# Linear attention and two MLPs on one core: 1 KB pieces for the loads of k and the first q

## The chip, the cores and the metric

The kernel runs on one core of one Trainium2 chip. The metric is device time in microseconds (us). The kernel before took 1558.11 us, the median of three runs that lay between 1558.07 and 1558.21. One execution of it was profiled.

## The reference

The kernel computes three layers for 8 batches of 576 tokens, 4608 tokens in all:

```python
kv  = np.einsum('bhsd,bhse->bhde', k, v)          # 8 batches, 8 heads, 576 tokens, head size 64
out = np.einsum('bhsd,bhde->bhse', q, kv)
rms = np.sqrt(np.mean(out * out, axis=-1, keepdims=True) + 1e-06)
x   = (out / rms * g_norm)                        # regrouped to x[4608, 512]
h   = x @ w_in                                    # first MLP, d_ff = 2048
g   = np.where(h >= 1, h, np.where(h <= -1, 0.0, (h + 1) ** 2 / 4.0))
x   = g @ w_out
h   = x @ w_in2                                   # second MLP
r   = np.maximum(h, 0.0)
return (r * r) @ w_out2
```

Inputs are float32, except that the weights lie in memory as 64-bit floats, which the kernel reads as pairs of 32-bit integers and narrows itself.

## The kernel before

**Layout.** Activations are held transposed: features on the 128 partitions, tokens along the row. d_model = 512 is 4 chunks of 128, d_ff = 2048 is 16 chunks of 128, counted f = 0 to 15. A pair of heads (hp = 0 to 3) fills 128 partitions and is one chunk of x. A batch has 512 tokens in its main block and 64 left over. Tile names give layer, batch or chunk: x_0_3 is x of batch 0, pair 3; ph_0_4 is the product x·w_in of batch 0 for chunk f = 4; u_0_4 and gs_0_4 are what the activation makes of it; acc_0_2 is the third of the four output accumulators of batch 0; raw_0_7 and raw_1_7 are the loads of chunk 7 of w_in and of w_out (in the order's names raw1_0_0 is layer 1's, w_in, chunk 0).

**Precision.** A product of float32 values is done as three products of halves (hi·hi, hi·lo, lo·hi; mm3, L237). So every weight passes, after its load of 512 KB, through `narrow_w` (ACT Prelu L267, DVE shift L269, DVE combine L270) and `split_halves` (ACT cast L216, DVE subtract L184): on ACT two, on DVE three instructions of 512 columns for each chunk. x is split likewise (ACT L216, DVE L229), and so is the activation's result (gs, ACT L216 and DVE L229).

**The first 120 us.** All queues start empty. SP issues the loads of k, v and q of batch 0 pair by pair, with weights raw_0_0 and raw_0_1 between pairs 1 and 2. It issues in program order; each of its DMAs takes one of eight landing semaphores in turn, and waits until the DMA eight places ahead has landed. For each pair `kv_stage` forms kᵀv on PE (pkv, L478), `t_first` transposes q by PE (pt, L499 for the main blocks, L501 for the left-over tokens) and DVE copies it out (qT, L218); `o_first` makes q·kv (po, L510; ACT square L511; DVE L210), `r_first` the norm (pr, L533; ACT Ln L534 and Exp L536; several DVE steps; x split L216, L229). `keep_warm` (L1146) puts products on a dummy tile between these. After that the main loop runs over seven batches and 16 chunks f: `h_stage` (ph; ACT relu L704, ACT square L223, DVE L706 to u), `g_stage` (gs) and `out_stage` (acc). Batches 1 to 7 have their attention woven into the loop: DVE transposes their q (L552), PE does pkv (L478), po (L568) and pr (L600).

**Banks.** In batch 0, ph of the chunks f = 2 to 5 sits in the PSUM banks of the accumulators acc_0_0 to acc_0_3. The first product of acc_0_c therefore waits until DVE (L706) has read ph_0_(c+2) for u_0_(c+2).

**What sets the order.** Up to about 714 us the order on each engine is not that of the code: a scheduler arranges the instructions by its own reckoning of when their inputs are there. Loads on SP keep their program order up to small shifts. From there to the end runs the second MLP with a reduced number of products (L877), in an order that the code fixes.

**The places of the change.** `load_kv` loads k and v of every batch and pair in one DMA each of 256 KB. Partition p holds the tokens 4p to 4p+3 of both heads. v lies on the partition as (head, token, 64): four tokens of a head follow each other in memory and on the partition. k lies as (token, head, 64), so that a token's two heads are 128 contiguous columns. `load_first` lays q of batch 0 out as k. In `t_first` one transposition then takes a token index c of both heads, 128 columns, at once.

Of the kernel before, what the change touches and what calls it, by code (L numbers as in the profile page):

```python
# [76 lines left out]
def linear_attention_rms_two_mlps(  # L77
# [12 lines left out]
    nc = tc.nc  # L90
    B, H, S, D = q.shape
    NT, DM = out.shape
    DFF = w_in1.shape[1] // 2
    P = 128
# [3 lines left out]
    TB = 512  # L98
    MR = TB // P
# [86 lines left out]
    ident = ap2.tile([P, P], F32, tag="q", name="ident")  # L186
# [218 lines left out]
    def load_kv(b, hp):  # L405
        h0 = 2 * hp
        if b > 0:

            r = rests[turn[b, hp] % len(rests)]
            kvr[b, hp] = (r[:, 0], r[:, 1])  # L410
        for n, src in enumerate((k, v)):
            pool, tag = (ep, "e") if (b, hp) == (0, NP - 1) else (st, "st")
            t = pool.tile([P, TB], F32, tag=tag, name=f"{'kv'[n]}_{b}_{hp}")
            rows = src[b, h0 : h0 + 2, :TB, :].rearrange("h (p r) d -> p h r d", r=MR)
            if n == 0:

                t = t.rearrange("p (r h d) -> p r h d", h=2, r=MR)
                nc.sync.dma_start(t, rows.rearrange("p h r d -> p r h d"))
            else:
                t = t.rearrange("p (h r d) -> p h r d", h=2, r=MR)  # L420
                nc.sync.dma_start(t, rows)
            kvm.setdefault((b, hp), []).append(t)
            if b > 0:
                rest = src[b, h0 : h0 + 2, TB:, :].rearrange("h p d -> p h d")
                nc.sync.dma_start(kvr[b, hp][n][:REM], rest)
# [14 lines left out]
    def load_first():  # L440


        left = wp.tile([REM, 2, H, D], F32, tag="w0_7", name="kvr0")
        qr = wp.tile([REM, H, D], F32, tag="w1_6", name="qr0")
        for hp in range(NP):
            load_kv(0, hp)
            heads = slice(2 * hp, 2 * hp + 2)
            kvr[0, hp] = (left[:, 0, heads, :], left[:, 1, heads, :])
            pool, tag = (ep, "e") if hp == NP - 1 else (st, "st")
            t = pool.tile([P, TB], F32, tag=tag, name=f"q_0_{hp}")  # L450
            t = t.rearrange("p (c h d) -> p c h d", h=2, c=MR)
            rows = q[0, 2 * hp : 2 * hp + 2, :TB, :].rearrange("h (p c) d -> p c h d", p=P)
            nc.sync.dma_start(t, rows)
            qs[0, hp] = [t[:, c] for c in range(MR)] + [qr[:, heads, :]]
            if hp == 1:
                for f in range(2):
                    load_w(1, f, 0)
            if hp == 0:
                for d, src in ((left[:, 0], k), (left[:, 1], v), (qr, q)):
                    nc.scalar.dma_start(d, src[0, :, TB:, :].rearrange("h p d -> p h d"))  # L460
                for j in range(2):
                    nc.scalar.dma_start(
                        gvec[j * D : (j + 1) * D, :], g_norm.rearrange("(d o) -> d o", o=1)
                    )

    def kv_stage(b, *hps):
        ps = bank(b, f"pkv_{b}_{hps[0]}")
        for n, hp in enumerate(hps):
            kt, vt = kvm.pop((b, hp))
            r = kvr.pop((b, hp))  # L470


            for c in range(MR + 1):
                for j in range(2):
                    s = slice(j * D, (j + 1) * D)
                    d = slice(n * P + j * D, n * P + (j + 1) * D)
                    lhs, rhs = (kt[:, c, j], vt[:, j, c, :]) if c < MR else (r[0][:, j], r[1][:, j])
                    nc.tensor.matmul(ps[s, d], lhs, rhs, start=c == 0, stop=c == MR)  # L478
        for n, hp in enumerate(hps):
            for j in range(2):  # L480
                s = slice(j * D, (j + 1) * D)
                d = slice(n * P + j * D, n * P + (j + 1) * D)
                if b == 0:
                    copy(engine("kv_hi", b), kv0[s, hp, s], ps[s, d])
                    continue
                if (b, hp) in WHOLE:
                    copy(engine("kv_hi", b), kvw[s, hp % 2, s], ps[s, d])
                    continue
                t = kvbd[turn[b, hp] % len(kvbd)]
                copy(engine("kv_hi", b), t[s, 0, s], ps[s, d])  # L490
                nc.vector.tensor_tensor(t[s, 1, s], ps[s, d], t[s, 0, s].bitcast(F32), ALU.subtract)

    def t_first(hp):
        qT = scratch(hp, "qT")
        q5 = qs[0, hp]
        for half in range(2):
            ps = bank(0, f"pt_0_{hp}_{half}")
            for c in range(2):
                nc.tensor.transpose(ps[:, c * P : (c + 1) * P], q5[2 * half + c], ident)  # L499
            rest = slice(half * (REM // 2), (half + 1) * (REM // 2))  # L500
            nc.tensor.transpose(ps[:, 2 * P : U], q5[MR][rest], ident[rest, rest])  # L501
            copy(engine("q_hi", 0), qT[:, half], ps[:, :U])
        hl[0, hp] = qT
# [774 lines left out]
```

## Time and profile before

| | |
|---|---|
| median of three runs | 1558.11 us |
| profiled execution | 1558.01 us |
| its span | 1556.1 us (1.9 us lie around it) |
| PE busy | 1546.0 us, 99% of the span |
| DVE busy | 1134.4 us, 73% |
| ACT busy | 975.8 us, 63% |
| DMA | 327,520 packets, 368.23 MB, mean 237 GB/s; 196,976 packets under 512 bytes |
| loads of k (main blocks) | 32 of 256 KB |
| loads of q of batch 0 | 4 of 256 KB |

Times are microseconds from the start of the span. An engine's busy time counts its own instructions; PEld, the load of stationary operands, runs beside PE. The chain of waits follows the work that ended last back to the start and says by which engine each stretch of it was set. In the timeline a bracket behind an instruction gives the idle time ahead of it on its engine and what ended this.

### The profile page before, as it was taken

The page shows a single profiled execution, that of the slowest core. Times are in us where ns is not written, and L with a number is a line of the kernel's source. Part 1 is how long each engine was busy: PE and PEld are TensorE (multiplying, and loading weights), DVE is VectorE, ACT ScalarE, POOL GpSimd, SP SyncE. Part 2 cuts the span into 40 slices and gives each one's busy share as a digit, 9 for nine tenths or more (in the row PEclk, how much of TensorE's full clock was granted, in tenths as well). Part 3 has the DMA queues.
Part 4 walks back from the last instruction along what each step waited for, and adds up shares of the span by engine and source line. Part 5 has one row for each costly group of instructions (what it writes and reads, how often), then busy time and mean ns, then how long its engine had stood idle before and what let it go on. Part 6 is the DMA issues. An engine that isn't in the chain of part 4 may idle for free.

```text
span 1556.1 us, 22351 instructions
## 1 busy us (share of the span) xinstructions
PE 1546.0 (99%) x7727; PEld 1283.7 (82%) x7729; DVE 1134.4 (73%) x2000; ACT 975.8 (63%) x1833; POOL 20.4 (1%) x38
## 2 busy tenths in 40 slices
PE   9999999999999999999999999999999999999999
PEld 5787888888888888888888888888888888888898
DVE  6986886877877786754587558778965596568666
ACT  5977766767666676765575466456646663666364
POOL 0000000000000000000000000000000000000000
PEclk9999999999999999999999999999999999999999
DMA  9666899996877967935676877696876676877797
GB/s 288 193 220 187 273 321 281 303 312 197 273 250 239 284 208 228 294 95 173 192 245 196 221 218 248 197 239 197 259 224 206 209 235 198 241 252 217 209 333 310
DMA packets 327520, 368.23 MB, mean 237 GB/s; under 512 B 196976, under 2 KB 222576, under 8 KB 327408
## 3 DMA queue, kind: packets, MB, share of 16 engines
q1 hardware_dynamic: 295360, 308.60, 66.8%
q10 hardware_dynamic: 32048, 58.20, 10.0%
q8 instruction: 61, 1.00, 0.3%
q14 instruction: 51, 0.42, 0.1%
HBM read 282.59 MB, written 84.15 MB: 236 GB/s over the span
## 4 chain that ended last, share of the span: by engine, by line
PE 97%; ACT 1%; DVE 1%; DMA 1%; issue 0%; SPq 0%; DVEq 0%; ACTq 0%
PE po L877 27%; PE ph L877 27%; PE acc L237 20%; PE ph L237 19%; PE pkv L478 1%; PE po L237 1%; PE pr L600 1%; DMA v<-in_v_dram 0%; PE pwarm L1146 0%; ACT raw L267 0%; ACT w L216 0%; DMA ws<-wsd 0%; PE pr L533 0%; DVE t L518 0%; DVE w L184 0%; PE po L510 0%
## 5 line engine op out<-in xcount | busy, mean ns | idle before, releaser
L877 PE MATMUL ph<-x,ws 128*128 128x512 f32 (+1 forms) x2016 | 422.6, 371 | 0.7 <-DMA ws<-wsd 0.7
L877 PEld LDWEIGHTS ph<-x,ws 128*128 128x128 f32 x2016 | 355.9, 188 | 66.4 <-DVE h L934 0.9
L877 PE MATMUL po<-t,ws 128*128 128x512 f32 x1680 | 381.6, 389 | 0.0
L877 PEld LDWEIGHTS po<-t,ws 128*128 128x128 f32 x1680 | 315.4, 188 | 65.4
L237 PE MATMUL ph<-x,w 128*128 128x512 f32 x1344 | 329.4, 392 | 1.2 <-ACT w L216 0.5
L237 PEld LDWEIGHTS ph<-x,w 128*128 128x128 f32 x1344 | 248.8, 188 | 54.1 <-ACT w L216 1.4
L806 DVE TENSOR_TENSOR t<-g,t 128x512 fp32r<-128x512 f32 (+1 forms) x288 | 183.6, 643 | 90.1 <-ACT t L216 84.5
L216 ACT CAST t<-g 128x512 fp32r<-128x512 f32 (+1 forms) x288 | 166.6, 585 | 101.8 <-DVE t L806 49.6
L237 PE MATMUL acc<-gs,w 128*128 128x512 f32 x696 | 173.0, 392 | 1.6 <-DVE u L706 1.6
L237 PE MATMUL acc<-gs,wt 128*128 128x512 f32 x648 | 157.9, 391 | 0.0
L237 PEld LDWEIGHTS acc<-gs,w 128*128 128x128 f32 x696 | 128.6, 188 | 27.8 <-DVE u L706 2.0
L934 DVE TENSOR_TENSOR h<-ph,e 128x512 f32<-128x512 f32 (+1 forms) x144 | 92.8, 646 | 68.3 <-PE ph L877 60.8
L237 PEld LDWEIGHTS acc<-gs,wt 128*128 128x128 f32 x648 | 120.1, 188 | 24.3
L704 ACT ACTIVATE u<-ph,halfb 128x512 f32<-128x512 f32 x112 | 77.3, 691 | 91.2 <-PE ph L237 88.7
L706 DVE SCALAR_TENSOR_TENSOR u<-u,ph 128x512 f32<-128x512 f32 x112 | 76.4, 682 | 53.6 <-ACT u L223 53.1
L941 ACT ACTIVATE h<-h 128x512 f32<-128x512 f32 (+1 forms) x120 | 70.3, 586 | 63.0 <-DVE h L934 58.3
L927 DVE TENSOR_TENSOR e<-ph,e 128x512 f32<-128x512 f32 (+1 forms) x96 | 61.3, 644 | 48.3 <-PE ph L877 47.4
L229 DVE TENSOR_TENSOR gs<-u,gs 128x512 fp32r<-128x512 f32 x112 | 76.9, 687 | 22.8 <-ACT gs L216 22.2
L216 ACT CAST gs<-u 128x512 fp32r<-128x512 f32 x112 | 69.8, 623 | 37.8 <-DVE u L706 34.7
L942 ACT ACTIVATE g<-h 128x512 f32<-128x512 f32 (+1 forms) x120 | 70.7, 589 | 3.2
L223 ACT ACTIVATE u<-u 128x512 f32<-128x512 f32 x112 | 70.9, 633 | 1.2 <-ACT u L704 0.3
L216 ACT CAST x<-xr 128x512 fp32r<-128x512 f32 (+1 forms) x84 | 49.1, 585 | 35.0 <-DVE xr L857 17.6
(134 smaller groups left out, 1533.0 us busy)
## 6 DMA issues: line engine op xcount, KB each, us to landing
ws<-wsd SPq DMA_DIRECT2D x336, 512.0 KB, 4.3
wsd<-s ACTq DMA_DIRECT2D x96, 512.0 KB, 4.9
wt<-wsd SPq DMA_DIRECT2D x54, 512.0 KB, 5.5
raw<-in_moe_w_in_dram SPq DMA_DIRECT2D x32, 512.0 KB, 6.0
raw<-in_moe_w_out_dram SPq DMA_DIRECT2D x32, 512.0 KB, 6.3
xr<-x1d SPq DMA_DIRECT2D x36, 256.0 KB, 4.8
out_dram<-ov SPq DMA_DIRECT2D x142, 64.0 KB, 3.7
wsd<-w SPq DMA_DIRECT2D x17, 512.0 KB, 4.7
```

The source lines that it names most:

```text
L216: return e.copy(dst, src)
L223: e.activation(dst, src, AF.Square)
L229: lo = engine(op + "_lo", phase).tensor_tensor(t[:, 1, :], src, t[:, 0, :].bitcast(F32), ALU.subtract)
L237: nc.tensor.matmul(dst, wt(a), xt(c), start=first and n == 0, stop=last and n == 2)
L704: nc.scalar.activation(u, ps, AF.Relu, bias=halfb, scale=0.5)
L706: nc.vector.scalar_tensor_tensor(u, u, 1.0, ps, op0=ALU.min, op1=ALU.max)
L806: engine2(op + "_lo").tensor_tensor(t[:, 1, :], src, t[:, 0, :].bitcast(F32), ALU.subtract)
L877: nc.tensor.matmul(ps, wt(a), xt(c), start=first and n == 0 and i == 0, stop=last and n == len(lhs) - 1 and i == 2, skip_group_check=True,)
L927: nc.vector.tensor_tensor(e[i, p], bank, e[i, 1], ALU.add)
L934: nc.vector.tensor_tensor(h, bank, add, ALU.add)
L941: nc.scalar.activation(u, h, AF.Relu)
L942: nc.scalar.activation(g, u, AF.Square)
```

## The change

k of all batches and q of batch 0 are laid out as v: (head, token, 64). A DMA of them is then made of pieces of 1 KB (four tokens of one head) where it was made of pieces of 256 bytes (one token of one head). The products for kᵀv take their stationary operand from the new place; there are as many as before, of the same shape. In `t_first` the two heads of a token are no longer next to each other; 16 transpositions of 128x128 (4 pairs, 2 halves, 2 token indices) become 32 products with the identity as moving operand, one for each head, with 64 columns of q stationary and an output of 64 partitions by 128. The left-over tokens are transposed as before.

```diff
@@ load_kv
-            if n == 0:
-                t = t.rearrange("p (r h d) -> p r h d", h=2, r=MR)
-                nc.sync.dma_start(t, rows.rearrange("p h r d -> p r h d"))
-            else:
-                t = t.rearrange("p (h r d) -> p h r d", h=2, r=MR)
-                nc.sync.dma_start(t, rows)
+            t = t.rearrange("p (h r d) -> p h r d", h=2, r=MR)
+            nc.sync.dma_start(t, rows)
@@ load_first
-            t = t.rearrange("p (c h d) -> p c h d", h=2, c=MR)
-            rows = q[0, 2 * hp : 2 * hp + 2, :TB, :].rearrange("h (p c) d -> p c h d", p=P)
+            t = t.rearrange("p (h c d) -> p h c d", h=2, c=MR)
+            rows = q[0, 2 * hp : 2 * hp + 2, :TB, :].rearrange("h (p c) d -> p h c d", p=P)
             nc.sync.dma_start(t, rows)
-            qs[0, hp] = [t[:, c] for c in range(MR)] + [qr[:, heads, :]]
+            qs[0, hp] = [t[:, :, c] for c in range(MR)] + [qr[:, heads, :]]
@@ kv_stage
-                    lhs, rhs = (kt[:, c, j], vt[:, j, c, :]) if c < MR else (r[0][:, j], r[1][:, j])
+                    lhs, rhs = (kt[:, j, c, :], vt[:, j, c, :]) if c < MR else (r[0][:, j], r[1][:, j])
@@ t_first
-                nc.tensor.transpose(ps[:, c * P : (c + 1) * P], q5[2 * half + c], ident)
+                for j in range(2):
+                    d = slice(j * D, (j + 1) * D)
+                    src = q5[2 * half + c][:, j]
+                    nc.tensor.matmul(ps[d, c * P : (c + 1) * P], src, ident, start=True, stop=True)
```

The new code also moves instructions that it does not name. The second MLP's part is in the same order as before; the part under the scheduler is not. Line numbers of the new kernel are a few lower: L704 there is L706 here, L550 is L552, L516 is L518, L519 and L520 are L521 and L522, L473 is L478, L566 is L568, L598 is L600.

First place: the start of DVE, behind its memsets. pt_0_0_0 and pt_0_0_1 are the two halves of the first pair's transposed q in PSUM, kv0 the copy of kᵀv, d1_0_0 the first step on the first weight chunk. Before:

```order
L218 COPY qT_0_0_235<-pt_0_0_0_236 128x288
L218 COPY kv0_126<-pkv_0_0_222 64x64 x2
L1159 TENSOR_SCALAR gvec_122<-gvec_122 128x1
L218 COPY qT_0_0_235<-pt_0_0_1_241 128x288
L218 COPY kv0_126<-pkv_0_1_252 64x64 x2
L210 TENSOR_SCALAR o_0_0_283<-po_0_0_1_288,gvec_122 128x288
L269 TENSOR_SCALAR d1_0_0_297<-raw1_0_0_151 128x512
```

And now:

```order
L269 TENSOR_SCALAR d1_0_0_305<-raw1_0_0_151 128x512
L218 COPY kv0_126<-pkv_0_0_222 64x64 x2
L1157 TENSOR_SCALAR gvec_122<-gvec_122 128x1
L218 COPY qT_0_0_235<-pt_0_0_0_236 128x288
L218 COPY qT_0_0_235<-pt_0_0_1_243 128x288
L218 COPY kv0_126<-pkv_0_1_256 64x64 x2
```

The first weight step stands ahead of all of the first pair's copies, where six of these stood ahead of it.

Second place: DVE around gs_0_2 and u_0_4, some 55 us into the run; d and w with two numbers are weight chunks on their way, d_1_5 of w_out and d_0_7 of w_in. Before:

```order
L706 SCALAR_TENSOR_TENSOR u_0_2_654<-u_0_2_654,ph_0_2_641 128x512
L552 STREAM_TRANSPOSE qT_0_565<-q_0_558 128x576
L184 TENSOR_TENSOR w_1_4_638<-d_1_4_635,w_1_4_638 128x2x256
L229 TENSOR_TENSOR gs_0_2_671<-u_0_2_654,gs_0_2_671 128x512
L269 TENSOR_SCALAR d_1_5_677<-raw_1_5_520 128x512
L706 SCALAR_TENSOR_TENSOR u_0_3_696<-u_0_3_696,ph_0_3_683 128x512
L270 SCALAR_TENSOR_TENSOR d_1_5_677<-raw_1_5_520,d_1_5_677 128x512
L706 SCALAR_TENSOR_TENSOR u_0_4_780<-u_0_4_780,ph_0_4_767 128x512
```

And now, the end of that stretch:

```order
L269 TENSOR_SCALAR d_1_6_777<-raw_1_6_606 128x512
L519 SCALAR_TENSOR_TENSOR t_0_728<-t_0_728,wk_1_0_579 128x576
L184 TENSOR_TENSOR w_0_7_638<-d_0_7_635,w_0_7_638 128x2x256
L269 TENSOR_SCALAR d_0_8_681<-raw_0_8_632 128x512
L520 TENSOR_TENSOR t_0_728<-wk_1_0_580,t_0_728 128x576
L270 SCALAR_TENSOR_TENSOR d_0_8_681<-raw_0_8_632,d_0_8_681 128x512
L270 SCALAR_TENSOR_TENSOR d_1_6_777<-raw_1_6_606,d_1_6_777 128x512
L229 TENSOR_TENSOR x_1_0_716<-t_0_728,x_1_0_716 128x512
L184 TENSOR_TENSOR w_0_8_684<-d_0_8_681,w_0_8_684 128x2x256
...
L184 TENSOR_TENSOR w_1_6_780<-d_1_6_777,w_1_6_780 128x2x256
...
L704 SCALAR_TENSOR_TENSOR u_0_4_796<-u_0_4_796,ph_0_4_783 128x512
```

u_0_4 stood four places behind gs_0_2 (the last row shown of before) and stands 20 places behind it now, with work on the weight chunks 5 to 9 and on the norm of batch 1's first pair in between.

Third place: PE from the middle of the first accumulators. Before:

```order
L237 MATMUL acc_0_1_849<-gs_0_0_587,w_1_0_494 128x512 x3
L237 MATMUL acc_0_1_849<-gs_0_1_625,w_1_1_501 128x512
L237 MATMUL acc_0_2_850<-gs_0_0_587,w_1_0_494 128x512 x3
L237 MATMUL acc_0_1_849<-gs_0_1_625,w_1_1_501 128x512 x2
L237 MATMUL acc_0_2_850<-gs_0_1_625,w_1_1_501 128x512 x3
```

And now:

```order
L237 MATMUL acc_0_1_865<-gs_0_2_687,w_1_2_531 128x512 x3
L473 MATMUL pkv_1_746<-v_1_586,k_1_583 64x64 x8
L473 MATMUL pkv_1_746<-rest_128 64x64 x2
L566 MATMUL po_1_0_837<-qT_1_761,kvw 128x288
L566 MATMUL po_1_1_850<-qT_1_761,kvw 128x288
L237 MATMUL ph_0_7_992<-x_0_0_217,w_0_7_638 128x512 x3
...
L598 MATMUL pr_1_0_966<-wk_1_1_759,ones 128x288
L598 MATMUL pr_1_1_969<-wk_1_1_759,ones 128x288
L237 MATMUL acc_0_2_866<-gs_0_0_603,w_1_0_510 128x512 x3
```

Between acc_0_1 and acc_0_2, PE now does the attention of batch 1's second pair and the four groups of three products of ph_0_7 (the first of the four groups is shown); the same rows stood later before.

## Rows read from the trace of the kernel before

**Rows 1.** Chain of waits, shares by engine.

```profile
PE 97%; ACT 1%; DVE 1%; DMA 1%; issue 0%; SPq 0%; DVEq 0%; ACTq 0%
```

**Rows 2.** Windows: us, PE, PEld, DVE, ACT, POOL busy; clock, DMA, GB/s.

```profile
0.00:50.00 50.00, 46.08 (x265) 29.13 (x267) 36.41 (x83) 32.43 (x63) 3.68 (x14) 1.00 0.94 274
10.00:40.00 30.00, 28.12 (x165) 18.31 (x167) 25.57 (x56) 21.21 (x43) 1.75 (x4) 1.00 0.99 308
...
150.00:200.00 50.00, 50.00 (x263) 41.30 (x263) 39.68 (x75) 37.07 (x75) 2.18 (x3) 1.00 0.85 267
```

**Rows 3.** PE timeline, 52 to 68 us: start, duration, engine, work, idle before.

```profile
54.31 0.96 PE L237 MATMUL acc<-gs,w 128*128 128x512 f32 x3 [1.56 <-DVE u L706]
57.81 4.27 PE L237 MATMUL acc<-gs,w 128*128 128x512 f32 x17
```

**Rows 4.** Timelines of DVE and ACT in the first 40 us.

```profile
10.06 0.46 DVE L218 COPY qT<-pt 128x288 f32<-128x288 f32 x1 [7.89 <-PE pt L501]
...
20.10 0.78 ACT L536 ACTIVATE y<-y,expb 128x576 f32<-128x576 f32 x1
...
39.82 0.68 DVE L229 TENSOR_TENSOR x<-t,x 128x512 fp32r<-128x512 f32 x1
```

**Rows 5.** DMA by window: weights 10.3 to 12.3, then k, 15.6 to 16.4.

```profile
DMA packets 652, 0.65 MB, mean 326 GB/s; under 512 B 15, under 2 KB 652, under 8 KB 652
...
DMA packets 780, 0.20 MB, mean 249 GB/s; under 512 B 776, under 2 KB 780, under 8 KB 780
```

**Rows 6.** SP timeline, 7 to 18 us: two issues of two loads.

```profile
7.78 0.92 SPq L249 DMA_DIRECT2D raw<-in_moe_w_in_dram  x2
...
16.27 1.24 SPq L249 DMA_DIRECT2D raw<-in_moe_w_in_dram  x2
```

**Rows 7.** DMA issues at 7.8, 16.3, 17.0 us: KB, us to landing.

```profile
raw<-in_moe_w_in_dram SPq DMA_DIRECT2D x1, 512.0 KB, 4.9
...
raw<-in_moe_w_in_dram SPq DMA_DIRECT2D x1, 512.0 KB, 6.4
...
raw<-in_moe_w_in_dram SPq DMA_DIRECT2D x1, 512.0 KB, 8.1
```

**Rows 8.** DVE timeline, 53 to 66 us.

```profile
53.58 0.68 DVE L706 SCALAR_TENSOR_TENSOR u<-u,ph 128x512 f32<-128x512 f32 x1
54.18 0.77 DVE L552 STREAM_TRANSPOSE qT<-q 128x576 f32<-128x576 f32 x1
54.87 0.65 DVE L184 TENSOR_TENSOR w<-d,w 128x512 fp32r<-128x512 f32 x1
55.44 0.68 DVE L229 TENSOR_TENSOR gs<-u,gs 128x512 fp32r<-128x512 f32 x1
56.04 0.42 DVE L269 TENSOR_SCALAR d<-raw 128x512 int32<-128x512 int32 x1
56.38 0.68 DVE L706 SCALAR_TENSOR_TENSOR u<-u,ph 128x512 f32<-128x512 f32 x1
...
61.17 0.82 DVE L518 SCALAR_TENSOR_TENSOR t<-pr,t 128x288 f32<-128x288 f32 x2 [0.69 <-ACT t L223]
62.02 0.76 DVE L521 SCALAR_TENSOR_TENSOR t<-t,wk 128x576 f32<-128x576 f32 x1
62.70 0.68 DVE L229 TENSOR_TENSOR gs<-u,gs 128x512 fp32r<-128x512 f32 x1
```

**Rows 9.** Pieces of the critical chain, 40 to 80 us: start, duration, work.

```profile
62.08 0.73 PE pkv L478 x20
...
65.99 0.97 PE po L568 x4
...
72.45 0.97 PE pr L600 x4
73.43 2.76 PE ph L237 x12
```

**Rows 10.** Groups by line, PE to 56 us: busy and mean ns, idle before.

```profile
L499 PE MATMUL pt<-ident,q 128*128 128x128 f32 x16 | 3.5, 290 | 0.0
```

## Prediction

> **What bounds the kernel now.** I read the chain of waits first: PE sets 97% of it [rows 1]. So the time changes only where PE waits or does more. The windows say where that is. From 150 us on PE is busy 50.00 of 50 us with DVE at 39.68 and ACT at 37.07; in the first 50 us it is busy 46.08, and between 10 and 40 us DVE has 25.57 busy us of 30 [rows 2]. The front is thus a race of DVE, ACT and DMA to give PE its first x and weights, and PE fills it with dummy products, so that its busy share there is no measure of use. Then the PE timeline around the first accumulators shows the one large late wait: 1.56 us at 54.31, ended by DVE's u [rows 3]. That is u_0_2, whose ph holds the bank of acc_0_0. Last I read DVE's timeline around it: one instruction behind the other, no idle time [rows 8]. DVE is the engine to watch, and the change moves instructions on it.
>
> **Terms.** The sum is made on the profiled execution, 1558.01 us (span 1556.1 plus 1.9), 0.1 below the median of the runs.
>
> *1. Loads.* A window inside a weight load, pieces of 1 KB, moves 326 GB/s; one inside a load of k, pieces of 256 bytes (776 of 780 packets under 512 bytes), 249 GB/s [rows 5]. A load of 256 KB takes 1.05 us at 249 and 0.80 at 326, 0.25 less. Batch 0 has four of k and four of q: 2.0 us less in the first 19 us, and 1.0 us less (two of each) ahead of the first weight raw_0_0. Packets fall by 36 loads times 768 = 27,648. The other 28 loads of k lie under a PE that is never idle [rows 2]: worth nothing.
> raw_0_0 lands at 7.78 + 4.9 = 12.7 us [rows 6, 7], so at 11.7 afterwards. I credit none of the 2.0 us by itself, because what follows is DVE's queue, which takes its own time (term 2); the bounds of the credit are 0 and −2.0.
> The Trainium skill agrees on the direction: "DMA: Bandwidth & Descriptors", section "Why small descriptors are slow (HBM only)", puts 11 cycles on a 256-byte piece, 8 of them for data. By that page a load would gain 1.05 x (1 − 8/11) = 0.29 us, eight of them 2.3 us, as an estimate; the rows' 0.25 is used.
>
> *2. DVE's start.* Before, DVE begins the first pair's copies at 10.06 and ends x_0_3 at 39.82 + 0.68 = 40.50 [rows 4]. Now the first weight step stands first, so DVE stands until raw_0_0 is there, 11.7, with the first copies behind it, and po_0 and pr_0 of PE behind these. From there DVE has the same 25.6 busy us [rows 2]: 37.3 without a wait. Following the new order I find two places where DVE must wait: about 1.5 us ahead of the copy of the third kᵀv (its product stands on PE behind pr of the first pair and two dummy products), and about 1.8 us ahead of the second pair's norm (ACT stands at the weights raw_0_2 and raw_0_3 first). Together 40.6 to 40.7 where it was 40.50: +0.2. These two waits are estimates from the order and the durations; a wait that does not come gives −3, one that doubles +3, and DVE's 4.4 idle us of 30 in 10 to 40 us are there to swallow either.
>
> *3. acc_0_0.* A transposition of 128x576 (one for each later pair of heads) now stands ahead of u_0_2 on DVE; start to start it costs 0.69 (54.18 to 54.87) [rows 8]. u_0_2 ended at 54.26 [rows 8]; now 54.26 + 0.2 + 0.69 = 55.15. So acc_0_0 starts at about 55.2 instead of 54.31, which by itself would be +0.9. But PE has in the meantime po and pr of batch 1's first pair out of the way, 2 x 0.97, as the later ones of the same shapes [rows 9], which it did before between 54.31 and 57.81.
>
> *4. acc_0_2.* PE now does 13 products of acc_0_0 and acc_0_1 (4.27/17 = 0.25 each as listed, 0.23 start to start: 2.76/12 [rows 3, 9]): 55.2 + 3.0 = 58.2. Five products with gs_0_2 follow (DVE has that at 55.15 plus u_0_3 and the two steps on a weight chunk and gs itself, 0.60 + 0.34 + 0.60 + 0.60 = 57.3): 1.15. Then pkv 0.73, po 0.97, the twelve of ph_0_7 2.76, pr 0.97 [rows 9]; PE stands at acc_0_2 at 58.2 + 6.6 = 64.8.
> acc_0_2 needs u_0_4. On DVE it is the 20th behind gs_0_2. Start to start [rows 8]: eleven of 512 columns with two operands at 0.60 are 6.6, four shifts at 0.34 are 1.4, the transposition 0.69, the two halves of the first norm step 0.82, two of 576 columns 1.35 (0.68 for one, 62.02 to 62.70): 10.8. u_0_4 is done at 57.3 + 10.8 = 68.1. PE waits 3.3 us.
> PE has then done 18 products of acc, pkv, po, pr and ph_0_7 and stands at 68.1. Before, it had six products of acc done at 57.81 [rows 3], and the same set would be complete at 57.81 + 12 x 0.23 + 0.73 + 0.97 + 2.76 + 0.97 = 66.0. So **+2.1 us** for terms 2 to 4. Since DVE stays full behind u_0_4 and PE has nothing it could do faster, I take it to stay to the end. Bounds: if u_0_4 is early, PE is not held at all and has at 64.8 what before it had at 66.0, −1.2; if DVE also waits for ACT on the way (the row of that norm step shows 0.69 of it [rows 8]) or runs later by the waits of term 2, up to +4.
> What hid u_0_4 before was its place four behind gs_0_2; that cover is gone. Behind the waiting acc_0_2 on PE stands all the rest of the batch, and no other engine can use the time: DVE is the one waited for.
>
> *5. More products on PE.* 16 transpositions become 32 products. The rows have 16 transpositions at 290 ns, 4.6 us in sum, 3.5 without overlap [rows 10]. No row has the new shape. The nearest is pkv: ten products of 64 moving columns in 0.73 us [rows 9], 0.073 each; with 128 columns twice that, 0.146, and 32 of them 4.7 us. So +0.1 to +1.2; were the two heads to run side by side, 2.3 us, a gain of 2.2. I take 0 for the end time, since they lie before 28 us where dummy products and waits for DVE surround them; without that cover it is what stands here.
>
> Sum: 1558.01 + 0 (loads) + 2.1 (terms 2 to 4) + 0 (term 5) = **1560.1 us**.
>
> **Rivals.** 0.2% of the time, 3.1 us, is about what a measurement of this kernel can tell from no change.
> *The saving shows.* The start is bound by the loads, x_0_3 comes earlier by what the pieces save, and the reordering is worth nothing: 1558.0 − 2.0 = 1556.0. For it: DMA engines are 99% busy from 10 to 40 us [rows 2]. Against it: DVE is 25.57 of 30 busy there, and the time at which a weight lands is not the time at which DVE gets to it. With a shorter norm chain on top it could pass −3.1. The Trainium skill is on this side: "Perfetto Trace Analysis", section 'What "DMA-bound" means', says that for such kernels large descriptors are what matters. By that rule the 2.0 us come back; the row of DVE speaks against its case being this one.
> *ACT held by loads (slower).* In the new order ACT takes raw_0_2 and raw_0_3 ahead of Ln and Exp of the second pair. They land at 16.27 + 6.4 = 22.7 and 17.0 + 8.1 = 25.1 [rows 6, 7], less 2.0: 20.7 and 23.1. Exp then starts not before 23.7, where a comparable one starts at 20.10 [rows 4]: +3.6, of which term 2 has 0.2. If neither DVE's idle time nor the dummy products absorb it, 1558.0 + 2.1 + 3.4 = 1563.5. It decides from the point where 4.4 idle us of DVE [rows 2] are used up.
> *Nothing.* u_0_4 comes by a shorter way than I sum, or PE makes the 2.1 us good out of small waits behind: 1558.0, give or take 0.7.
> *Dear products.* If a float32 product with the identity costs four times the transposition, 16 x 3 x 0.29 = 13.9 us more of PE in the first 28 us, up to 1571.9 if none is hidden. The pkv row speaks against it. The Trainium skill has the ratio: "TensorE: Matmul & The Clock Gate", section "Terms", calls the transposing mode 4 times faster for float32. No run here shows that yet.
> That the pieces do not change is excluded: the load's tile and source both run (head, token, 64) now.
>
> **How the numbers follow.** Forecast 0.43, the saving shows 0.16, ACT held 0.22, nothing 0.16, dear products 0.03. The likeliest's own range is 1558.8 to 1561.6. The range for eight in ten goes from 1555.9, the saving's time, to 1563.6, that of ACT held; some two in ten lie beyond. Faster by over 0.2% (under 1555.0): 0.08, half of the saving's case. Slower by over 0.2% (over 1561.2): nearly all of ACT held, the dear products, and a sixth of the forecast's case: 0.32. Within: 0.60.
>
> **What would show it.** DVE's first instruction behind its memsets is the step on raw_0_0, with its wait ended by ACT or a DMA at 11 to 13 us; PE idles some 3 us ahead of acc_0_2 between 60 and 70 us, ended by DVE's u (line 704 of the new kernel); u_0_2 ends at about 55; packets are 27,648 fewer; from 150 us on PE is busy 50 of 50 as before. I am wrong if PE has no such wait or has its largest elsewhere, if the start of acc_0_0 moves by over 2 us, or if the new products have more than 6 us in the trace.

## The result and the profile after

The changed kernel takes 1569.53 us, the median of runs between 1568.02 and 1572.88, where the kernel before took 1558.07 beside it: 1.0083 times as long, 95% interval 1.0071 to 1.0094. The forecast was 1560.1 with a range to 1563.6. The profiled execution has a span of 1567.5 us, 11.4 more than before.

The chain of waits of the kernel after, by engine [rows 1]:

```profile
PE 94%; DMA 3%; ACT 2%; DVE 1%; issue 0%; SPq 0%; ACTq 0%; DVEq 0%
```

PE's share of the chain was 97%. The three points are no measure of the time lost, because the chain also follows a DMA while PE is still at work. PE's windows say where time is lost; first three stretches as in [rows 2], then the rest of the first two layers (PE, PEld, DVE, ACT, POOL busy, granted clock, DMA share, GB/s):

```profile
0.00:50.00 50.00, 46.38 (x305) 29.73 (x306) 34.66 (x80) 30.81 (x61) 3.28 (x14) 1.00 0.96 314
10.00:40.00 30.00, 29.43 (x209) 18.88 (x208) 23.59 (x53) 20.78 (x42) 0.71 (x3) 1.00 0.98 325
150.00:200.00 50.00, 50.00 (x265) 41.66 (x264) 38.09 (x71) 34.38 (x69) 2.81 (x2) 1.00 0.94 292
150.00:400.00 250.00, 246.39 (x1286) 204.49 (x1285) 189.83 (x353) 169.27 (x337) 9.32 (x11) 0.99 0.88 276
400.00:720.00 320.00, 317.43 (x1642) 263.80 (x1641) 224.11 (x410) 209.43 (x414) 4.56 (x10) 0.99 0.70 219
```

The last two rows of the kernel before:

```profile
150.00:400.00 250.00, 250.00 (x1310) 207.68 (x1310) 196.74 (x365) 176.11 (x351) 7.95 (x11) 1.00 0.89 280
400.00:720.00 320.00, 320.00 (x1659) 266.25 (x1658) 226.53 (x413) 210.62 (x415) 6.37 (x9) 1.00 0.74 227
```

A PE that was never idle between 150 and 720 us now is, 3.6 and 2.6 us. Idle time is not all, so I compare progress: at the time t at which PE of the kernel before has done a certain number of columns (without the dummy products, the transpositions of the front and the narrow products for kᵀv), how much later has this kernel done as many? This is the lag. Up to 150 us it also moves with the order of the work itself (with the products for kᵀv counted in, it is 3.8 at 100 us, not 4.5), so where the order is a new one the readings rest on 200 us and later.

```
us later than before, at t =   25   40   60   70  100  200  250  275  490  515 1200
kernel after                  0.5  4.0  0.4  4.3  4.5  2.0  2.0  7.4  7.5 11.9 12.3
```

The front costs 2.0 us by 200 us. Two places behind it cost 5.4 (at 260 us) and 4.4 (at 500). Near the end 0.9 comes back, since a wait of 0.72 us of the kernel before at 1500 us is gone.

PE of the kernel after at these two places, the first and then the second (start, duration, idle before and what ended it):

```profile
259.35 1.29 PE L237 MATMUL acc<-gs,w 128*128 128x512 f32 x5
264.25 0.40 PE L237 MATMUL po<-qT,kvbd 128*128 128x288 f32 x1 [3.61 <-ACT qT L216]
264.49 1.00 PE L237 MATMUL acc<-gs,w 128*128 128x512 f32 x2
...
502.43 0.40 PE L237 MATMUL po<-qT,kvbd 128*128 128x288 f32 x1 [2.57 <-ACT qT L216]
```

Both times q·kv of a later batch stands at ACT's cast of its transposed q, with the accumulators' products queued behind it. At 260 us ACT itself stood. Its timeline:

```profile
260.14 0.60 ACT L216 CAST s<-s 128x512 fp32r<-128x512 f32 x1
263.12 0.37 ACTq L176 DMA_DIRECT2D wsd<-s  x1
263.53 0.67 ACT L216 CAST qT<-qf 128x576 fp32r<-128x576 f32 x1 [2.79 <-DMA wsd<-w]
```

And the chain there:

```profile
252.49 10.56 DMA wsd<-w
...
263.07 0.02 ACTq L176
```

wsd are stores of prepared second-MLP weights. ACT issues one; its landing semaphore was last used by a store that SP issued at 252.49 and that landed at 263.05; ACT stands until then, and the cast that PE needs is behind the store. In the kernel before that cast stands ahead of the store, and PE does the same po without a wait (ACT, then PE):

```profile
256.24 0.68 ACT L216 CAST qT<-qf 128x576 fp32r<-128x576 f32 x1 [0.85 <-DVE qf L557]
257.59 0.37 ACTq L176 DMA_DIRECT2D wsd<-s  x1
...
257.84 0.29 PE L237 MATMUL po<-qT,kvbd 128*128 128x288 f32 x1
```

At 500 us it is DVE: the transposition qf stands behind work on a weight tile wf.

```profile
491.02 5.18 DMA wf<-wsd
...
496.29 0.69 DVE wf L340
...
500.90 0.78 DVE qf L555
```

In the kernel before DVE does the transposition ahead of its step on that tile:

```profile
489.95 0.77 DVE L557 STREAM_TRANSPOSE qf<-q 128x576 f32<-128x576 f32 x1
...
499.25 0.69 DVE L340 TENSOR_TENSOR wf<-wf 128x512 f32<-128x512 f32 x1 [2.21 <-DMA wf<-wsd]
```

After the pause PE is also slower for a while. Windows directly behind it, and a little later:

```profile
264.30:267.50 3.20, 3.20 (x10) 2.55 (x11) 2.60 (x4) 3.20 (x8) 0.00 (x0) 0.54 1.08 386
268.00:272.00 4.00, 4.00 (x21) 3.35 (x20) 1.37 (x2) 1.83 (x5) 0.00 (x0) 1.00 0.88 235
```

A granted clock of 0.54, about the lower level of 1.2 GHz, for some 3.2 us: ten products are listed in them, and 21 in the 4.0 us a little later. By this clock I estimate some 1.5 us on top of the 3.6 of waiting, 5.1 of the 5.4 in all.

The front: DVE's start [rows 4] and what ends its waits:

```profile
11.72 0.43 DVE L269 TENSOR_SCALAR d<-raw 128x512 int32<-128x512 int32 x1 [9.55 <-DMA raw<-in_moe_w_in_dram]
13.21 0.15 DVE L1157 TENSOR_SCALAR gvec<-gvec 128x1 f32<-128x1 f32 x1 [0.70 <-DMA gvec<-in_g_norm_dram]
20.96 0.22 DVE L218 COPY kv<-pkv 64x64 f32<-64x64 f32 x1 [2.40 <-PE pkv L473]
41.84 0.69 DVE L229 TENSOR_TENSOR x<-t,x 128x512 fp32r<-128x512 f32 x1
```

PE around the first accumulators [rows 3, 9], DVE's u_0_2 (the third u of the batch) and u_0_4 [rows 8], and the new products [rows 10]; these are 64 records, two for each of the 32:

```profile
56.97 4.39 PE L237 MATMUL acc<-gs,w 128*128 128x512 f32 x18
61.28 0.69 PE L473 MATMUL pkv<-v,k 128*64 128x64 f32 x16
62.61 1.24 PE L566 MATMUL po<-qT,kvw 128*128 128x288 f32 x4 [0.52 <-ACT kvw L216]
63.77 3.29 PE L237 MATMUL ph<-x,w 128*128 128x512 f32 x12
68.71 1.24 PE L598 MATMUL pr<-wk,ones 128*128 128x288 f32 x4 [1.65 <-ACT wk L208]
70.10 6.21 PE L237 MATMUL acc<-gs,w 128*128 128x512 f32 x26 [0.16 <-DVE u L704]
```

```profile
56.23 0.68 DVE L704 SCALAR_TENSOR_TENSOR u<-u,ph 128x512 f32<-128x512 f32 x1
...
69.37 0.68 DVE L704 SCALAR_TENSOR_TENSOR u<-u,ph 128x512 f32<-128x512 f32 x1
```

```profile
L497 PE MATMUL pt<-ident,q 128*64 128x128 f32 x64 | 5.7, 286 | 0.0
```

The transfers [rows 5 to 7]. A window from 12 to 14 us, with loads of k, v and q and the end of a weight load, now moves 379 GB/s, where one inside a load in pieces of 256 bytes moved 249. It is the best of those read: three windows from 5 to 11 us move 315 to 330. From 5 to 16 us as a whole it is 348 GB/s, where it was 298. SP's weight issues start at 5.01 and 13.21 instead of 7.78 and 16.27:

```profile
DMA packets 853, 0.76 MB, mean 379 GB/s; under 512 B 113, under 2 KB 853, under 8 KB 853
```

```profile
5.01 2.75 SPq L249 DMA_DIRECT2D raw<-in_moe_w_in_dram  x2
...
13.21 0.92 SPq L249 DMA_DIRECT2D raw<-in_moe_w_in_dram  x2
```

The packets fall to 299,873, by 27,647.

### The profile page after: what moved, and what is told of

It is laid out like the page before. It is cut to its first block, busy times and chain, and to the rows that moved or that the text cites. A ratio compares the mean times of both kernels' runs of the same rounds, so it can differ in the third digit from the quotient of the medians.

```text
span 1567.5 us, 22414 instructions
## 1 busy us (share of the span) xinstructions
PE 1551.6 (99%) x7777; PEld 1288.4 (82%) x7777; DVE 1134.3 (72%) x2000; ACT 973.7 (62%) x1833; POOL 19.1 (1%) x38
## 2 busy tenths in 40 slices
DMA packets 299873, 368.24 MB, mean 235 GB/s; under 512 B 160112, under 2 KB 194928, under 8 KB 299760
## 4 chain that ended last, share of the span: by engine, by line
PE 94%; DMA 3%; ACT 2%; DVE 1%; issue 0%; SPq 0%; ACTq 0%; DVEq 0%
PE po L875 27%; PE ph L875 27%; PE acc L237 18%; PE ph L237 17%; PE po L237 1%; PE pkv L473 1%; DMA x1d<-ev 1%; PE pr L598 1%; DMA wsd<-w 1%; DMA k<-in_k_dram 0%; ACT w L216 0%; ACT raw L267 0%; DMA wf<-wsd 0%; DMA gvec<-in_g_norm_dram 0%; ACT u L702 0%; PE pwarm L1144 0%
## 5 line engine op out<-in xcount | busy, mean ns | idle before, releaser
L704 DVE SCALAR_TENSOR_TENSOR u<-u,ph 128x512 f32<-128x512 f32 x112 | 76.4, 682 | 50.3 <-ACT u L223 49.9
```

The costliest lines, as they stand in the source:

```text
L704: nc.vector.scalar_tensor_tensor(u, u, 1.0, ps, op0=ALU.min, op1=ALU.max)
```

## Experiments

My theory: the two pauses come from the order in which the scheduler now writes the work behind 200 us; the pieces and the products as such cost little. One rival: the transfers, which now run earlier or in other pieces, make the stores and tiles land late. Another: the products themselves cost the time, in PE or by what they hold up. In the expectations this is theory A (A1 in the runs that move rows); A2, B, C and D are the rivals, and E is about what delays the front in the order of before. Where an order is said to be held, the instruction sequence of each engine from the named kernel is written into the program and kept:

```diff
+        keep_order(tc, nc, _mybir)   # each engine: its instructions in the order listed
```

Each was measured beside the kernel before, in 4 to 11 executions, and one execution was profiled. Lag is the measure of the table above, from the profiled execution:

```
                                     ratio   interval          lag 25   60  100  200  250  275  515 1200
new pieces, order for old pieces     1.0050  1.0037 to 1.0062    2.6  3.2  3.2  3.2  9.6  9.6  9.6  9.7
old pieces, order of after           1.0080  1.0066 to 1.0093    1.1  1.0  5.1  3.4  3.3  7.7 12.4 12.3
products only                        1.0042  1.0030 to 1.0055    0.5  1.0  1.0  1.0  6.2  6.2  6.8  7.0
after, two rows moved                1.0031  1.0019 to 1.0043    1.4  1.4  5.4  2.9  2.9  7.6  8.3  8.6
whole change, order of before        1.0019  1.0010 to 1.0028    2.7  2.6  2.6  2.6  2.6  2.6  2.5  2.6
products, order of before            1.0015  1.0006 to 1.0024    1.2  1.2  1.2  1.2  1.2  1.2  1.1  1.2
after, three places moved            1.0035  1.0023 to 1.0047    0.7  0.7  4.7  2.3  2.3  5.1  5.7  5.6
pieces of k only                     1.0054  1.0041 to 1.0066   -0.9 -0.7  0.7 -0.6  0.0  5.6  7.3  8.5
change, order of before, g first     1.0053  1.0040 to 1.0065    9.2  9.2  9.1  9.1  9.4  9.4  9.3  9.5
pieces of k, order of before         1.0014  1.0006 to 1.0023    1.0  1.0  1.0  0.9  0.9  0.9  0.8  0.9
the same, g first                    1.0009  1.0000 to 1.0018    0.7  0.7  0.7  0.6  0.6  0.6  1.1  1.2
the same, g by GpSimd                1.0006  0.9997 to 1.0015    3.0  3.0  2.9  2.9  2.9  2.9  3.1  3.1
```

**New pieces, the order for old pieces.** The whole change, held to the order that the scheduler gives the same program when its loads are in 256-byte pieces.

> The changed kernel (1 KB pieces, 32 products), each engine held to the order that the scheduler gives the same program with 256-byte pieces, which up to the first 40 us and a handful of rows is that of before. Theory A (the loss is the order's): lag 0 to 0.5 us behind x_0_3, no pauses near 260 and 500 us, about 1558 us, down to 1556 if the faster loads of the first 20 us show. Theory B (the faster loads themselves collide with other transfers): the pauses near 260 and 500 us stay, about 1567 to 1570 us.

Measured 1564.58 us, between the two forecasts. The pauses at 260 and 500 are gone, as my theory had it, but there is one of 3.42 us in the trace at 208, the same kind of wait:

```profile
212.17 0.61 PE L237 MATMUL po<-qT,kvbd 128*128 128x288 f32 x1 [3.42 <-ACT qT L216]
```

So the order decides where the pause lies; this other order is not free of one. The lists that were held tell how much the size of the pieces moves: to get this one, for 256-byte pieces, at least 107 rows of the order of before have to be moved (each transposition's place taken by its two products), and at least 1,164 rows of the order of after.

**Old pieces, the order of after.** The reverse: only the loads are turned back, one 256-byte piece for each token and head; the products read as in the kernel after, so they take other tokens' values.

```diff
-            nc.sync.dma_start(t, rows)
+            u = t.rearrange("p (r h d) -> p r h d", h=2, r=MR)
+            nc.sync.dma_start(u, rows.rearrange("p h r d -> p r h d"))
```

The cut shows the load of k; that of the first q is turned back likewise.

> The changed kernel's program in its own order, but k and the first q are moved in 256-byte pieces (token-major, so that heads and tokens lie in other columns than the products take them from: the values are wrong, the work is the same). Theory A: the lag at 200 us about +2 to +3, pauses near 260 and 500 us, about 1569 us (1567 to 1573). Theory B: no pauses, about 1559 to 1561 us.

Measured 1569.5 us, that of the kernel after, with both pauses:

```profile
264.41 0.40 PE L237 MATMUL po<-qT,kvbd 128*128 128x288 f32 x1 [2.39 <-ACT qT L216]
...
502.99 0.40 PE L237 MATMUL po<-qT,kvbd 128*128 128x288 f32 x1 [2.95 <-ACT qT L216]
```

In the order of after the size of the pieces makes no difference of the end time that these intervals show. So the transfers in their new pieces are not the cause of the pauses. Nor does holding an order show a cost: this run is held and has small pieces, the kernel after is not held and has large ones, and both take 1569.5 us.

**Products only.** The 32 products, loads as before, the scheduler free.

```diff
-                nc.tensor.transpose(ps[:, c * P : (c + 1) * P], q5[2 * half + c], ident)
+                for j in range(2):
+                    d = slice(j * D, (j + 1) * D)
+                    src = q5[2 * half + c][:, j]
+                    nc.tensor.matmul(ps[d, c * P : (c + 1) * P], src, ident, start=True, stop=True)
```

> Before with one edit: 32 products with the identity for the 16 transpositions, loads in 256-byte pieces. The forecast's term 5 says 0 (range -1 to +1.2 us): about 1558 us. Theory C (the products are dear or delay x): +2 us or more, and with the order of before nearly kept no pauses in the middle in either case.

Measured 1564.01 us: lag 1.0 up to 200 us, then a pause at 206. Neither forecast had a pause here.

```profile
209.93 0.40 PE L237 MATMUL po<-qT,kvbd 128*128 128x288 f32 x1 [3.39 <-ACT qT L216]
```

Here too ACT stood at a cast waiting for a store (4.82 us). The store was issued by ACT at 199.79 instead of 195.63 and landed at 208.03. It is the pause of the run with new pieces and the order for old pieces, where ACT stood 4.83 us at the same cast; so it comes with either size of pieces. This run does not separate what of it is the moved rows and what is the later store.

**After, two rows moved.** In the order of after, on ACT the cast of the first pause's q is put ahead of the store issue, and on DVE the step on the weight tile and the four behind it are put behind the transposition of the second pause's q.

> The changed kernel in its own order with two moves: on ACT the cast of qT for batch 3, pair 1 goes ahead of the one store's issue that stood before it; on DVE the five rows that begin with wf_13 (which waits for a load) go behind qf and qT of batch 5, pair 3. Theory A1 (the pauses are work queued behind an instruction that waits for a DMA): the pauses of 3.6 and 2.6 us go with the slow products behind them, about 1569.5 - 5.3 - 4.4 = 1560 us (1559 to 1564). Theory A2 (PE pays for the transfers being late, wherever the queues stand): the pauses move some rows on, 1567 to 1570 us.

Measured 1562.46 us, inside what theory A1 gave. The profiled execution is the slowest of the six (1565.56; the others took 1560.83 to 1562.77), so its lag of 8.6 is not that of the median. The pause at 500 is gone, and PE passes:

```profile
499.79 0.84 PE L237 MATMUL acc<-gs,wt 128*128 128x512 f32 x3
500.47 0.29 PE L237 MATMUL po<-qT,kvbd 128*128 128x288 f32 x1
```

The one at 260 stays (2.58 us): the cast no longer waits for the store, but for DVE, whose transposition stands in a queue that had stood 5.86 us for a weight tile.

```profile
254.09 0.69 DVE L340 TENSOR_TENSOR wf<-wf 128x512 f32<-128x512 f32 x1 [5.86 <-DMA wf<-wsd]
```

One wait had covered another. So the second pause is shown to be the place of those five rows of DVE; the first is not that of the one row on ACT alone.

**After, three places moved.** Also that DVE step and its followers are put behind the transposition at 260, and ACT's two casts and store behind the cast of q.

> The changed kernel in its own order with two places changed: near 500 us as before (the rows from wf_13 go behind qf and qT of batch 5, pair 3), and near 260 us now on DVE as well (the rows from wf_9, which waits for a load, go behind qf and qT of batch 3, pair 1; on ACT the two casts and the store that hang on them go behind the cast of qT). Theory A1 (work queued behind an instruction that waits for a DMA): both pauses go, 1562.5 - 4.6 = 1558 us (1557 to 1560). Theory A2 (PE pays for late transfers wherever the queues stand): another pause of 3 us or more, 1561 to 1566 us.

Measured 1562.43 us. Both pauses are gone, lag 2.3 through 250, but waits of 0.23, 0.91 and 1.01 come between 266 and 278:

```profile
270.42 0.40 PE L598 MATMUL pr<-s2lo,ones 128*128 128x288 f32 x1 [0.91 <-DVE s2lo L584]
...
277.79 0.69 PE L473 MATMUL pkv<-v,k 128*64 128x64 f32 x16 [1.01 <-DVE t L516]
```

I take it that what was put behind is now late in its turn. The lag ends at 5.6, against 12.3 in the kernel after. The mechanism of theory A1 held, its time did not: 1557 to 1560 us was forecast, and the time lies in the range of A2, without a pause of 3 us.

**Whole change, order of before.** Each transposition is replaced in place by its two products; everything else stands as before on every engine.

> The whole change (1 KB pieces, 32 products), with every engine held to the order of before, row by row; each transposition's place is taken by its two products. Theory A (the loss is all order): no pauses of over 1 us behind 130 us; front lag 0 to 1.5 us; 1557 to 1559 us. Theory D (what is late are transfers, by which landing semaphore and when, and the order is only one cause): a pause of 3 to 4 us near 206 us as in the two runs in nearly the same order, 1563 to 1566 us.

Measured 1560.53 us. From 22 us to 1450 the lag is flat, and no instruction of PE waits between 150 and 720:

```profile
150.00:400.00 250.00, 250.00 (x1311) 207.85 (x1310) 194.37 (x361) 175.08 (x348) 7.95 (x11) 1.00 0.88 280
400.00:720.00 320.00, 320.00 (x1660) 266.16 (x1660) 227.58 (x416) 210.82 (x418) 6.04 (x9) 1.00 0.73 228
```

This shows the order to be the cause: the same work and the same transfers take some 8 to 10 us less in the order of before. The median is 3.2 us above the kernel before beside it where that of the kernel after was 11.5, and the lag ends at 2.6 instead of 12.3. What is left, 2.6 of lag, lies ahead of 22 us; theory A had allowed 1.5 and 1559 us, and the pause near 206 us of theory D did not come.

**Products, order of before.** Only the 32 products, in place.

> Before with the 32 products alone, 256-byte pieces, every engine held to the order of before. Theory A: 1557 to 1559 us, front lag 0 to 1 us (products 11.4 us of PE records in the first 28 us would otherwise show). Against the run with the whole change in this order it gives what the 1 KB pieces do by themselves: the forecast's -2.0 would make the other one 2 us faster; 0 if the data wait for DVE and ACT anyway.

Measured 1559.83 us; lag 1.2, flat. DVE waits 0.71 and 0.30 us for PE at the second pair:

```profile
14.96 0.46 DVE L218 COPY qT<-pt 128x288 f32<-128x288 f32 x1 [0.71 <-PE pt L504]
15.72 0.46 DVE L218 COPY qT<-pt 128x288 f32<-128x288 f32 x1 [0.30 <-PE pt L504]
```

The pause at 206 is gone, so it came with the moved rows, of which the later issue of the store is one. The products do cost something of themselves, by the lag a tenth of the whole and a little more than the 1 us that theory A allowed; the median lies 2.5 us above the kernel before beside it.

**Pieces of k only.** The loads of k in 1 KB pieces, q and its transposition as before, the scheduler free.

> Before with k in 1 KB pieces for all batches; q and its transpositions as before; order as the scheduler then makes it. Theory A (any edit redraws the order, and pauses come where a q·kv product stands behind a DMA's wait): lag at 150 us between -2 and +3, and the time is that plus 4 to 6 us for each pause, 1556 to 1570 us; each pause ends with a cast of qT or a copy of q. Theory B (the pieces by themselves): no new pauses, 1556 to 1558 us.

Measured 1565.84 us, as theory A had it: no lag at 250, then 3.68 us of waiting at 259 and the same stretch at the lower clock (0.50 from 264.3 to 267.7).

```profile
262.82 0.40 PE L237 MATMUL po<-qT,kvbd 128*128 128x288 f32 x1 [3.68 <-ACT qT L216]
```

**Pieces of k, order of before.**

> Before with k alone in 1 KB pieces, held to the order of before (its own order took 1565.8 us). Theory A: no pauses. Theory E: DVE stands for gvec by 0.5 to 2 us, lag 0.5 to 1.5 us, 1557.5 to 1559 us. If the saving of the loads shows: -1 us, 1556.3 us.

Measured 1560.15 us, no pause, lag 0.9: some 6 us less than with a free scheduler (2.5 us above the kernel before beside it, where that was 8.5). The lag is inside the range of theory E, the time is 1.2 us beyond it. The pieces of k are thus no gain even where nothing else moves. The lag again arises ahead of 22 us, and there DVE waits for g:

```profile
12.38 0.15 DVE L1154 TENSOR_SCALAR gvec<-gvec 128x1 f32<-128x1 f32 x1 [2.13 <-DMA gvec<-in_g_norm_dram]
```

The first loads, from issue to landing:

```
                         SP's issue of k  left-over q     g, second load   raw_0_0
before                   0.77 us          2.48 to  8.03   6.20 to  9.45    7.78 to 12.65
pieces of k, old order   0.45             2.27 to  8.58   7.38 to 12.27    5.05 to 11.28
kernel after             0.45             3.85 to 10.55   8.12 to 13.11    5.01 to 11.69
```

SP's issue of the first load in large pieces takes 0.45 us where it took 0.77, and SP reaches its next loads earlier. The eight landing semaphores are not SP's alone: SP and ACT take the same eight in turn (g's second load in the kernel after was issued at 8.12, when the semaphore's last user, a load of k by SP, had landed at 8.10). Of the small loads that ACT issues, which DVE and PE need first in the order of before, g's second goes out 1.2 and 1.9 us later and takes some 5 us to land instead of 3.25. I take the reason for the latter to be that it shares the DMA engines with weights that nobody waits for yet; no run separates this.

**The same, g first, and the change with g first.** ACT issues the loads of g ahead of the left-over tokens.

```diff
+                    nc.scalar.dma_start(gvec...)     # ahead of kvr and qr
```

> The same with the loads of g_norm issued first: the version that could beat both kernels. Theory E: no stand for gvec, and x and the weights come as early as the loads allow: lag -1 to 0 us, 1556 to 1557.5 us. If DVE's own work sets the end of the front whatever lands when: lag 0, 1557.3 us.

> The whole change held to the order of before, with one more edit: ACT issues the two small loads of g_norm ahead of the three loads of the left-over tokens. Theory E (in that order the 1 KB pieces cost 1.4 us because the quick large loads run ahead of the small loads that DVE's queue needs first; DVE stood 1.95 us for gvec): gvec lands by 7 us, DVE does not stand for it, lag at 100 us 0.7 to 1.2 us instead of 2.6, 1558.5 to 1559.5 us. If DVE then stands for the left-over q instead, or if the lag is from the contention of the first loads as such, lag and time stay at 2.6 and 1560.5 us.

With k alone 1558.35 us, lag 0.7: DVE no longer waits for g, but the left-over q lands at 10.22 (8.58 with g behind it), and neither forecast came (at most 1557.5). With the whole change 1565.53 and lag 9.1, beyond both forecasts: the left-over q can be issued only at 8.28, when the semaphore's last user has landed (8.26), lands at 14.89, and DVE starts with it.

```profile
15.28 0.46 DVE L218 COPY qT<-pt 128x288 f32<-128x288 f32 x1 [13.11 <-PE pt L499]
```

PE stood 2.89 and 2.22 us in this front, and its granted clock is 0.50, the lower level, from 11.5 to 21.8 us: eight records of the products then take 1.12 us, where they take 0.66 in the kernel after at a clock of 1.00. So one small load behind the semaphores, with the lower clock that follows the wait, costs more here than all pieces could give.

**The same, g by GpSimd.** With the pieces of k alone and the order of before, GpSimd's queue issues g.

```diff
-                    nc.scalar.dma_start(
+                    nc.gpsimd.dma_start(
```

> k in pieces of 1 KB, q's transposition as before, the order of before, and the two loads of g issued by GpSimd's queue instead of ScalarE's. If the 0.95 us by which PE lay behind in the run with k's pieces in the order of before came from the small loads that ScalarE issues too late (g waited for until 12.38 us), DVE does not wait for g here, the left-over q lands by 8.6 us, PE lies 0 to 0.5 us ahead of before from 22 us on, and the time is 1556.5 to 1557.7 beside 1557.7 of before. The rival: DVE's own work or a busy DMA sets the front, the lag stays 0.7 to 1.0 us at any place of g, and the time is 1558.3 to 1560.

Measured 1558.28 us beside 1557.18, no difference that this tells. g landed at 5.80 and 9.19 and is not waited for, yet the left-over q landed at 10.49 and the first q at 10.66 (7.35 with g on ACT), and DVE starts at 11.41:

```profile
11.41 0.46 DVE L218 COPY qT<-pt 128x288 f32<-128x288 f32 x1 [9.24 <-PE pt L496]
```

The profiled lag is 2.9, so the expectation is missed and its rival's lag is not right either (1.0 at most). But this execution is the slowest of the eleven (1560.98), and from 12.8 to 16.2 us its granted clock is 0.50; the lag of the median is not known. Why the q loads were slower is open. The last three versions with k's pieces cannot be ranked by their intervals, and none beats the kernel before.

## Why the prediction was wrong

*Term 1, the credit for the first loads.* raw_0_0 landed at 11.69 (11.7 computed), but by luck: SP issued it 2.8 us earlier, at 5.01, and it took 6.7 us to land instead of 4.9. The kernel after shows no credit. The estimate of 0.29 us a load that term 1 works out from the Trainium skill is too high by its own figures: with 3 cycles lost on each piece, four pieces of 256 bytes take 44 cycles and one of 1 KB takes 35, which makes 0.21 us. The rival in which the saving shows did not come: PE is ahead of before only with the pieces of k alone and a new order, by 0.6 at 200 us, and has lost that by 250. The Trainium skill's rule in "Perfetto Trace Analysis", section 'What "DMA-bound" means', would have given 2.0 us back for all eight loads, 1.0 for the four of k; with the order held, the pieces of k lose 0.9.

*Term 1, the other 28 loads, "under a PE that is never idle: worth nothing", and with it "I take it to stay to the end".* This is the step that failed. It put the stretch behind the first 70 us at nothing, since no edit names it, although the order was known to be another up to some 714 us; the new order was read for the front alone. The scheduler arranges that stretch by its reckoning of when loads are there, and the size of the pieces alone makes it write another order. The edit reached that stretch as moved rows, not as transfers: a cast behind a store issue, a transposition behind a tile. The two places cost 5.4 and 4.4 us, together 9.8, where the miss is 9.4 (1569.5 less 1560.1), and the largest wait of PE stood there, not at acc_0_2. Rows that I had read to be safe (PE 50.00 of 50) said that nothing waited in the order of before, not that there was slack in another.

*Term 2, DVE's start, +0.2.* The place was right, the size was not: x_0_3 ended at about 42.5 instead of 40.6 to 40.7. DVE started at 11.72 as computed, was busy 26.0 us up to there (25.6 computed) and stood 4.8 instead of 3.3: 2.40 for the third kᵀv (1.5 estimated), 0.54 ahead of the second pair's norm (1.8 estimated), and 0.70 for g and 0.48 for a transposition, which were not foreseen.

*Terms 3 and 4, +2.1 together.* The sum is met, 2.0 at 200 to 250 us, but by luck and not by its parts. DVE runs 1.8 to 2.0 us behind the computed times, about as late as x_0_3 is: u_0_2 ended at 56.91, not 55.15, and u_0_4 at 70.05, not 68.1. acc_0_0 started right behind u_0_2, at 56.97, 2.7 us later than before and beyond the 2 us at which I called myself wrong, with PE at other products until then. PE stood 2.3 us, not 3.3, and of these only 0.16 at acc_0_2; 0.52 and 1.65 were ended by ACT, ahead of po and pr. The lag was 4.3 at 70 us and fell to 2.0, which "PE has nothing it could do faster" had excluded; how PE made this good is not traced.

*Term 5, 0 for the products.* In place, they cost 1.2 us of lag, through DVE's wait for PE at the second pair. That this is the upper bound of the estimate is luck: 32 of them take 5.7 us in the trace, 2.2 more than the 3.5 of the transpositions, 0.18 each (0.146 estimated), and a transposition's two 0.36 against 3.5/16 = 0.22. Where the Trainium skill ("TensorE: Matmul & The Clock Gate", section "Terms") has a factor of 4, the two half-wide products that replace a transposition take 1.6 times its time; a float32 product of the transposition's own shape stands in no run here. The rival of dear products fell.

*ACT held by loads.* It did not come: raw_0_2 and raw_0_3 landed at 18.5 and 20.5 us (20.7 and 23.1 computed), the front's lag is 2.0, without the 3.4 more of that case, and the DMA waits that decided are those of stores and tiles behind 200 us.

By the lags of the profiled executions the runs show the sum as: order 9.7 us (12.3 less 2.6), products 1.2, pieces about 1 (the whole change in the order of before is 2.6, 0.4 above both). By the medians the three runs in the order of before lie 3.2, 2.5 and 2.5 us above the kernel before, so the shares of products and pieces are not settled; that of the order is.

What stays open: which of the moved rows make the waits at 266 to 278 in the version with three places moved; why the store in the run with products alone landed so late; and why the medians of those three runs in the order of before lie 0.6 to 1.6 us above what the lag of the profiled execution gives.

## What to carry to other kernels

Where a scheduler writes the order, an edit of a load is an edit of the whole program: compare the orders to the last stretch, and look in each for an instruction that the critical engine needs standing behind one that waits for a DMA. Then run the edit once with the old order held, to tell its own price from that of the order. Larger pieces pay only if what lands sooner is what is waited for; here the first weight landed 1.0 to 1.4 us sooner and the second load of g 2.8 to 3.7 us later, and none of the versions with g moved was a gain.

## What the runs showed of the hardware

A pause of PE of 3.6 us is followed by 3.2 us at a granted clock of 0.54 in which ten products run, and PE falls 5.4 behind in progress. In the change with g first, PE stood 2.89 and 2.22 us in the front and then worked at 0.50 up to 21.8 us. With three places moved, the waits at 260 to 280 are at most 1.01 us, and the granted clock there stays 1.00. And a DMA of one queue delays another's without sharing data: an issue on ACT waited until 263.05 for a store issued by SP at 252.49, because both used the same landing semaphore.
